# Attention on one core: the order of steps written over four rounds instead of two, with five bursts of V products

## The chip, the cores and the metric

The kernel runs on one core of a Trainium2 chip. The metric is the device time of one execution in microseconds. The median of three runs of the kernel before is 2798.07 us (2798.04 to 2798.45).

## The reference

Two attention blocks A and B with 32 heads of width 16 act on the same input x (2048 tokens, 512 features, fp32), each with its own weights, and their results are mixed by a gate of one number per token.

```python
qkv = transpose((x @ wqkv).reshape(B, S, 3, H, Dh), 2, 0, 3, 1, 4)
q, k, v = qkv[0], qkv[1], qkv[2]
p = softmax(einsum("bhqd,bhkd->bhqk", q, k) * Dh ** -0.5, axis=-1)
o = einsum("bhqk,bhkd->bhqd", p, v)
a = transpose(o, 0, 2, 1, 3).reshape(B, S, D) @ wo     # the same for b with its weights
g = sigmoid((x * gate_w).sum(-1, keepdims=True))
out = g * a + (1 - g) * b
```

## The kernel before

**Heads and rounds.** The 64 heads of A and B are worked through one after the other. A head has 16 rounds; a round is a tile of 128 keys against all 2048 queries. That makes 1024 rounds, and `r` counts them. Three kinds of work belong to them, each some rounds apart from the others:

- *Scores* (`score(r, c)`, step `e`): one matmul of 128 keys by 512 queries into a bank of `ps_st`, and one exponential on ScalarE from the bank to the tile `p` of the round. A round has four. Ahead of the exponential the maximum of each query over all keys must be known; it enters the matmul as two more rows of the operands (50 rows: 48 for the product, in which each number is split in two parts, and two for the maximum).
- *Maxima* (`max_plain`, `max_pair`, `max_rise`): another pass over the same products, 22 rounds ahead (`m = r + NT + LEAD`). A plain one (step `m`) is a matmul of 128 queries by 512 keys into a bank of `ps_m` and a reduction on VectorE into a column of `mxp`, the head's tile of partial maxima. In every second round two of the four are joined: `max_rise` (step `D`) puts the difference of two keys' products into a bank of `ps_st`, from which ScalarE makes its positive part, the tile `rise`; `max_pair` (step `A`) makes a product into `ps_m`, and VectorE adds `rise` and takes the maximum in one instruction.
- *V products* (`attend`, a digit): the exponentials times V, in quarters of a round (128 queries of each 512). Four matmuls stand side by side in the columns of the array, and the sums for a head gather in the one bank `acc`. A digit is a burst of so many quarters. When a head ends, ScalarE copies `acc` to `ev` and SyncE stores it to `od`.

**Pairs on the array.** Scores and maxima fill 48 or 50 of 128 rows, so `q_st` and `k_st` hold each head twice, at rows 0 and 64 (`HALVES`), and matmuls take the halves in turn (`rows()`, `turn`): two neighbours run at the same time. At each burst the turn is set back to the first half. `max_rise` always stands on the first half, which is where `x_st` lies.

**What sets the order.** The instructions of each engine are issued in the order of the program. The order is written out by hand as a string, `FULL`, of which each character is a step; the loop goes through it once for two rounds (`LATE` where no maxima are left). `ps_st` has four banks, `ps_m` three, `p` and `rise` have three and two buffers.

**Around the loop.** Before it stands the prologue with the projections and the first 24 rounds of maxima. In it `later` holds work with a round at which it is due: loads of V, the gate, and the output projection (`project_out`), issued ahead of the next burst. At a head's first round `load_stacks` loads the operands of the head after the next through SyncE's queue, ten DMAs. When the last maximum of a head is done, `max_split` reduces its `mxp` to `mrow` and `max_rows` transposes it and sends it through memory into the two further rows of `q_st`; two dictionaries say in which round.

Of the kernel before, what the change touches and what calls it, by code (L numbers as in the profile page):

```python
# [23 lines left out]
F32 = mybir.dt.float32  # L24
# [8 lines left out]
P = 128  # L33
# [4 lines left out]
NT = S // P  # L38
# [4 lines left out]
NH = 2 * H  # L43
ROUNDS = NH * NT
LEAD = 6
# [6 lines left out]
def gated_mha(ctx: ExitStack, tc: tile.TileContext, xT, x, wqkv_a, wo_a, wqkv_b, wo_b, gate_w, out):  # L52
    nc = tc.nc
    pe, act, dve, pool = nc.tensor, nc.scalar, nc.vector, nc.gpsimd
# [4 lines left out]
    small = ctx.enter_context(tc.tile_pool(name="small", bufs=2))  # L59
# [31 lines left out]
    def load_stacks(h, halves=HALVES):  # L91
        dma = nc.sync.dma_start
        s, hh = divmod(h, H)
        g, j = divmod(hh, HG)
        q, k = q_st[h % 3], k_st[h % 3]
        qs, ks, xs = qd[s][g], kd[s][g], xd[s][g]

        def pairs(t, step, n=S):
            v = t[0, j]
            return bass.AP(tensor=v.tensor, offset=v.offset, ap=[[n, DH], [step, 2], [1, n]])  # L100

        for b in halves:
            dma(k[b:b + 32].bitcast(F32), pairs(ks, HG * DH * S))
            dma(q[b:b + 32].bitcast(F32), pairs(qs, 0))
            dma(k[b + 32:b + 48].bitcast(F32), ks[0, j])
            dma(q[b + 32:b + 48].bitcast(F32), qs[1, j])
        if h and halves[-1] == HALVES[1]:
            x = x_st[h % 2]
            dma(x[:32].bitcast(F32), pairs(xs, HG * DH * 512, 512))
            dma(x[32:SC].bitcast(F32), xs[0, j])  # L110
# [5 lines left out]
    LOWEST = -3.4028234e38  # L116
    FIRST = NT + LEAD + 2
    mxp, rises = {}, {}
    turn = [0]

    def rows():
        turn[0] ^= 1
        return HALVES[1 - turn[0]]

    def scores_bank(m, c):
        h, t = divmod(m, NT)
        if h not in mxp:
            mxp[h] = small.tile([P, NT, 4], F32, name="mxp")
            if h:
                pool.memset(mxp[h][:, FIRST % NT if h == 1 else 0::2, 1:2], LOWEST)  # L130
        pool_ = ps_st if c == "rise" else ps_m
        ps = pool_.tile([P, 512], F32, name="ps_st" if c == "rise" else "ps_m")
        b = rows()
        q = q_st[h % 3]
        if c == "rise":
            assert b == 0
            k = x_st[h % 2][:]
        else:
            k = k_st[h % 3][b:b + SC, c * 512:(c + 1) * 512]
        pe.matmul(ps, q[b:b + SC, t * P:(t + 1) * P], k, start=True, stop=True)  # L140
        return ps, mxp[h][:, t]

    def max_plain(m, c):
        ps, o = scores_bank(m, c)
        dve.tensor_reduce(o[:, c:c + 1], ps, op=ALU.max, axis=AX.X)  # L145
# [3 lines left out]
    def max_rise(m):  # L149
        ps, _ = scores_bank(m, "rise")  # L150
        rises[m] = small.tile([P, 512], F32, name="rise")
        act.activation(rises[m], ps, AF.Relu)  # L152

    def max_pair(m):
        ps, o = scores_bank(m, 0)
        rise = rises.pop(m)
        dve.tensor_tensor_reduce(out=rise, in0=ps, in1=rise, scale=1.0, scalar=LOWEST,  # L157
                                 op0=ALU.add, op1=ALU.max, accum_out=o[:, 0:1])
# [3 lines left out]
    def max_split(h):  # L162
        parts = mxp.pop(h)
        m = small.tile([P, NT], F32, name="mrow")
        mp = small.tile([P, 2, NT], F32R, name="mparts")
        dve.tensor_reduce(m, parts, op=ALU.max, axis=AX.X)  # L166
        pool.tensor_copy(mp[:, 0], m)  # L167
        pool.tensor_tensor(mp[:, 1], m, mp[:, 0].bitcast(F32), op=ALU.subtract)
        mparts[h] = mp

    def max_rows(h):
        mt = small.tile([P, 32], F32, name="mt")
        dve.transpose(mt, mparts.pop(h).rearrange("p i t -> p (i t)").bitcast(F32))
        q = q_st[h % 3]
        r = md[h % 3]
        nc.sync.dma_start(r.rearrange("i (t a x) -> a (i t) x", a=4, x=32), mt)
        for b in HALVES:
            nc.sync.dma_start(q[b + SC:b + SC + 2].bitcast(F32), r)
# [4 lines left out]
    def score(r, c):  # L183
        h, kt = divmod(r, NT)
        if c == 0:
            pt[r] = pro.tile([P, S], F32, name="raw") if r < 2 else ppool.tile([P, S], F32, name="p")
        q, k = q_st[h % 3], k_st[h % 3]
        kk, cc = (4 * (kt % 4) + c, kt // 4) if h == NH - 1 else (kt, c)
        b = rows()
        ps = ps_st.tile([P, 512], F32, name="ps_st")  # L190
        pe.matmul(ps, k[b:b + SC + 2, kk * P:(kk + 1) * P], q[b:b + SC + 2, cc * 512:(cc + 1) * 512],  # L191
                  start=True, stop=True)
        act.activation(pt[r][:, c * 512:(c + 1) * 512], ps, AF.Exp, scale=SCALE)  # L193
# [12 lines left out]
    with tc.tile_pool(name="xs", bufs=1) as xs, tc.tile_pool(name="pro", bufs=2) as pro:  # L206
# [20 lines left out]
        def load_x(c, n):  # L227
            raw = pro.tile([P, KC, 512], F32, name="raw")
            for k in range(0, KC, n):
                nc.sync.dma_start(raw[:, k:k + n], xT[k * P:(k + n) * P, c * 512:(c + 1) * 512].rearrange(  # L230
                    "(k p) t -> p k t", p=P))
            return raw

        def split_x(c, n, raw):
            for k in range(0, KC, n):
                act.copy(xh[c][:, k:k + n], raw[:, k:k + n])  # L236
                dve.tensor_tensor(xl[c][:, k:k + n], raw[:, k:k + n], xh[c][:, k:k + n].bitcast(F32),
                                  op=ALU.subtract)
# [50 lines left out]
        def block(fn, i):  # L289
            if i < len(blocks):  # L290
                s, g, isk = blocks[i]
                fn(s, isk * DM + g * P, P)
# [5 lines left out]
        for c in range(1, NQ):  # L298
            split_x(c, 2, load_x(c, 2))
            if c < 3:  # L300
                block(load_w, c)
        ahead = [(m, c) for m in range(NT + LEAD + 2) for c in range(4)]

        def run_ahead():
# [25 lines left out]
        for t in range(NT):  # L330
# [6 lines left out]
            if t >= NT - 4:  # L337
                for c in range(2):
                    score(*divmod(2 * (t - NT + 4) + c, 4))
        turn[0] = 0  # L340
        max_rise(NT + LEAD + 2)
        assert not ahead and not pending


# [32 lines left out]
    e = core.tile([P, NT], F32, name="gate_e")  # L377
# [153 lines left out]
    later = {}  # L531
# [80 lines left out]
    def attend_next(n):  # L612
        while n:
            r, qa = divmod(done[0], 4)
            qb = min(4, qa + n)
            attend(r, qa, qb)
            done[0] += qb - qa
            n -= qb - qa

    FULL = "m3memeem3meAe2Dmeee"  # L620
    LATE = "e2ee2ee2ee2e"
    splits, rows_of = {}, {}

    load_stacks(2)
    for r in range(2, ROUNDS, 2):
        h, kt = divmod(r, NT)
        projects = []
        for rr in (r, r + 1):
            for fn, a in later.pop(rr, ()):
                if fn is project_out:  # L630
                    projects.append(a)
                else:
                    fn(*a)
        if kt == 0 and h + 2 < NH:
            load_stacks(h + 2)
        m = r + NT + LEAD
        plain = [(m, 2), (m, 3)] + [(m + 1, c) for c in range(4)]
        scored = 0
        for step in FULL if m < ROUNDS else LATE:
            if step == "e":  # L640
                score(r + scored // 4, scored % 4)
                scored += 1
            elif step == "m":
                max_plain(*plain.pop(0))
            elif step == "D":
                if m + 2 < ROUNDS:
                    max_rise(m + 2)
            elif step == "A":
                if m in rises:
                    max_pair(m)  # L650
                else:
                    max_plain(m, 0)
                    max_plain(m, 1)
            else:
                for a in projects:
                    project_out(*a)
                projects = []
                turn[0] = 0
                attend_next(int(step))
                if r in splits:  # L660
                    max_split(splits.pop(r))
                if r in rows_of:
                    max_rows(rows_of.pop(r))
        m += 1
        if m < ROUNDS and m % NT == NT - 1:
            splits[r + 2] = rows_of[r + 4] = m // NT
    attend_next(8)
    fill_only.append(True)
    for fn, *a in fill:
# [26 lines left out]
```

## Time and profile before

| | |
|---|---|
| median of three runs | 2798.07 us |
| the profiled execution | 2798.53 us, span 2796.8 us |
| TensorE busy | 2781.7 us (99%) |
| ScalarE busy | 2424.0 us (87%) |
| VectorE busy | 2363.1 us (84%) |
| GpSimd busy | 254.8 us (9%) |
| exponentials of the scores | 4088, 626 ns each by their records |
| plain maxima on VectorE | 3096, 683 ns each |
| granted TensorE clock | 0.999 |

PE is TensorE's matmuls, PEld its weight loads, ACT ScalarE, DVE VectorE, SP SyncE with its DMA queue (SPq). Records of one engine overlap where instructions follow each other closely, and ends of matmuls are modelled, so busy time alone does not say how much an engine has left; the distance between starts or ends does.

### The profile page before, as it was taken

Reading aid. Unit: us, or ns where it says so; the run is one execution under the profiler, and the core shown is the slowest. Engines: PE = TensorE matmul, PEld = TensorE weight load, DVE = VectorE, ACT = ScalarE, POOL = GpSimd, SP = SyncE. Lnnn points to the kernel's source line nnn. Section 1 sums busy time; section 2 is a strip of 40 time slices with the busy share of each in tenths; the row PEclk is TensorE's granted clock in tenths of the full one; section 3 lists DMA queues with packets and bytes.
Section 4 is the critical chain, followed back from the end, with each engine's and each line's share of the span. In section 5 each row is a group of like instructions: output and inputs, shape, how many; then the busy total and the mean of one; then the engine's idle time right before and its main releaser. Section 6 shows DMA issues by size and latency. Waiting matters only on the chain.

```text
span 2796.8 us, 65495 instructions
## 1 busy us (share of the span) xinstructions
PE 2781.7 (99%) x26176; PEld 1317.1 (47%) x26176; DVE 2363.1 (84%) x4431; ACT 2424.0 (87%) x4789; POOL 254.8 (9%) x456
## 2 busy tenths in 40 slices
PE   8999999999999999999999999999999999999999
PEld 7877544444444444444444445444444444444444
DVE  4155799999999999999999877899999999998774
ACT  3221799999999999999999977899999999998785
POOL 2010112110000000000100232000000001011201
PEclk9999999999999999999999999999999999999999
DMA  7673423333333223333432442332323333333302
GB/s 259 203 247 146 96 60 79 66 68 58 70 62 55 53 60 56 58 60 58 89 58 49 102 102 61 58 58 50 63 53 60 58 78 70 58 73 87 76 11 93
DMA packets 91126, 225.25 MB, mean 81 GB/s; under 512 B 24150, under 2 KB 34358, under 8 KB 78278
## 3 DMA queue, kind: packets, MB, share of 16 engines
q1 hardware_dynamic: 88262, 212.15, 34.0%
q0 software_dynamic: 2560, 8.91, 1.2%
q8 instruction: 206, 3.38, 0.5%
q14 instruction: 98, 0.80, 0.1%
HBM read 152.07 MB, written 68.94 MB: 79 GB/s over the span
## 4 chain that ended last, share of the span: by engine, by line
PE 98%; ACT 1%; DMA 0%; DVE 0%; SPq 0%; issue 0%
PE acc L589 38%; PE ps_m L140 26%; PE ps_st L191 13%; PE ps_st L140 8%; PE ps_st L251 6%; PE ps_st L281 3%; PE ps_m L475 3%; ACT p L193 1%; DMA raw<-in_xT 0%; PE ps_st L475 0%; PE ps_st L526 0%; PE ps_m L526 0%; DVE o_acc L527 0%; PE ps_m L513 0%; SPq L230 0%
## 5 line engine op out<-in xcount | busy, mean ns | idle before, releaser
L193 ACT ACTIVATE p<-ps_st 128x512 f32<-128x512 f32 x4088 | 2073.0, 626 | 82.7 <-PE ps_st L191 69.7
L145 DVE TENSOR_REDUCE mxp<-ps_m 128x1 f32<-128x512 f32 x3096 | 1949.8, 683 | 184.5 <-PE ps_st L191 135.2
L140 PE MATMUL ps_m<-k_st,q_st 48*128 48x512 f32 x3596 | 1353.9, 446 | 0.1
L191 PE MATMUL ps_st<-q_st,k_st 50*128 50x512 f32 x4096 | 1215.6, 426 | 0.0
L589 PE MATMUL acc<-p,vg 128*17 128x384 f32 (+1 forms) x16336 | 1182.8, 384 | 2.9 <-ACT ev L597 2.0
L140 PEld LDWEIGHTS ps_m<-k_st,q_st 48*128 48x128 f32 x3596 | 608.6, 183 | 550.0 <-DVE mxp L145 499.7
L191 PEld LDWEIGHTS ps_st<-q_st,k_st 50*128 50x128 f32 x4096 | 617.3, 184 | 200.3 <-ACT p L193 179.8
L589 PEld LDWEIGHTS acc<-p,vg 128*17 128x17 f32 x16336 | 313.9, 96 | 422.4 <-issue 399.6
L157 DVE CUSTOM_DVE_ANT_0 rise<-ps_m,rise 128x512 f32<-128x512 f32 x500 | 339.6, 679 | 0.0
L152 ACT ACTIVATE rise<-ps_st 128x512 f32<-128x512 f32 x500 | 301.8, 604 | 37.3
L140 PE MATMUL ps_st<-x_st,q_st 48*128 48x512 f32 x500 | 248.1, 496 | 0.0
L140 PEld LDWEIGHTS ps_st<-x_st,q_st 48*128 48x128 f32 x500 | 91.4, 183 | 211.6 <-ACT p L193 211.1
L167 POOL CAST mparts<-mrow 128x16 fp32r<-128x16 f32 x64 | 12.6, 197 | 1913.8 <-DVE mrow L166 1913.8
L254 ACT CAST part<-ps_st 128x512 fp32r<-128x512 f32 x64 | 37.4, 587 | 131.9 <-PE ps_st L251 117.0
L255 DVE TENSOR_TENSOR part<-ps_st,part 128x512 fp32r<-128x512 f32 x64 | 43.9, 690 | 90.3 <-ACT part L254 79.3
L475 PE MATMUL ps_m<-wo,ot 128*128 128x512 f32 (+1 forms) x354 | 91.0, 402 | 0.0
L284 ACT COPY v_st<-ps_st 128x512 f32<-128x512 f32 x32 | 18.8, 587 | 79.8 <-PE ps_st L281 70.3
L251 PE MATMUL ps_st<-xh,whi 128*128 128x512 f32 x256 | 73.0, 405 | 8.1 <-ACT xh L236 8.1
L475 PEld LDWEIGHTS ps_m<-wo,ot 128*128 128x128 f32 (+1 forms) x354 | 64.0, 188 | 20.3 <-DVE mxp L157 5.9
L251 PE MATMUL ps_st<-xh,wlo 128*128 128x512 f32 x256 | 69.9, 396 | 0.0
L251 PE MATMUL ps_st<-xl,whi 128*128 128x512 f32 x256 | 69.5, 394 | 0.0
L251 PEld LDWEIGHTS ps_st<-xh,whi 128*128 128x128 f32 x256 | 47.6, 191 | 24.7 <-ACT xh L236 10.4
(95 smaller groups left out, 814.4 us busy)
## 6 DMA issues: line engine op xcount, KB each, us to landing
k_st<-kd SPq DMA_DIRECT2D x128, 256.0 KB
q_st<-qd SPq DMA_DIRECT2D x128, 256.0 KB
qd<-part SPq DMA_DIRECT2D x32, 512.0 KB
kd<-part SPq DMA_DIRECT2D x32, 512.0 KB
k_st<-kd SPq DMA_DIRECT2D x128, 128.0 KB
q_st<-qd SPq DMA_DIRECT2D x128, 128.0 KB
od<-ev SPq DMA_DIRECT2D x63, 256.0 KB
vd<-v_st SPq DMA_DIRECT2D x32, 272.0 KB
```

What stands on the lines that cost most here:

```text
L140: pe.matmul(ps, q[b:b + SC, t * P:(t + 1) * P], k, start=True, stop=True)
L145: dve.tensor_reduce(o[:, c:c + 1], ps, op=ALU.max, axis=AX.X)
L152: act.activation(rises[m], ps, AF.Relu)
L157: dve.tensor_tensor_reduce(out=rise, in0=ps, in1=rise, scale=1.0, scalar=LOWEST, op0=ALU.add, op1=ALU.max, accum_out=o[:, 0:1])
L191: pe.matmul(ps, k[b:b + SC + 2, kk * P:(kk + 1) * P], q[b:b + SC + 2, cc * 512:(cc + 1) * 512], start=True, stop=True)
L193: act.activation(pt[r][:, c * 512:(c + 1) * 512], ps, AF.Exp, scale=SCALE)
L251: pe.matmul(ps, a[:, k], b[:, k], start=n == 0, stop=n == 3 * KC - 1)
L254: act.copy(pt[0][:, sl], ps)
L255: dve.tensor_tensor(pt[1][:, sl], ps, pt[0][:, sl].bitcast(F32), op=ALU.subtract)
L281: pe.matmul(ps, a[:, k, o:o + P], b[:, k], start=n == 0, stop=n == 3 * KC - 1)
L475: pe.matmul(ps, ot[a][:n, slot, sl], wt[b][:n, g], start=G == groups[0] and i == 0, stop=G == groups[-1] and i == 2)
L589: pe.matmul(acc[32 * c:32 * c + 17, qa * P:qb * P], v[:, 4 * a + c if final else kt, j], p[:, c * 512 + qa * P:c * 512 + qb * P], start=fi ...
```

## The change

The string `FULL` now covers four rounds with five bursts (3, 4, 3, 3, 3 quarters) in place of two rounds with three (3, 3, 2). The loop starts at round 2 as before and takes four rounds a pass, so a head is four passes and starts in the middle of one. Rises are made four and six rounds ahead of the pass's first maximum (`to_rise`), two of them with one score between, and the prologue makes two of them instead of one. What is due in the third and fourth round of a pass is issued at its ninth score (`due(r + 2)`). The stacks are loaded in the round after the first two of a head. `mxp` is made and its columns set (`new_maxima`) in the prologue for two heads and then eight rounds ahead of the head's first maximum, where it was made at its first use. `max_split` and `max_rows` go behind the first and the second burst of the pass that follows a head's last maxima.

```diff
+    def new_maxima(h):
+        mxp[h] = small.tile([P, NT, 4], F32, name="mxp")
+        if h:
+            pool.memset(mxp[h][:, FIRST % NT if h == 1 else 0::2, 1:2], LOWEST)
+
     def scores_bank(m, c):
         h, t = divmod(m, NT)
-        if h not in mxp:
-            mxp[h] = small.tile([P, NT, 4], F32, name="mxp")
-            if h:
-                pool.memset(mxp[h][:, FIRST % NT if h == 1 else 0::2, 1:2], LOWEST)
...
-        turn[0] = 0
-        max_rise(NT + LEAD + 2)
+        for i in range(2):
+            turn[0] = 0
+            max_rise(FIRST + 2 * i)
...
-    FULL = "m3memeem3meAe2Dmeee"
+    FULL = "mme3emmeem4meeemAe3emmeeem3meeemA3DeD"
...
+    load_stacks(2)
+    r = 2
+    while r < ROUNDS:
         m = r + NT + LEAD
-        plain = [(m, 2), (m, 3)] + [(m + 1, c) for c in range(4)]
+        order = FULL if m < ROUNDS else LATE
+        n = order.count("e") // 4
+        due(r)
+        if r % NT == 2 and r // NT + 2 < NH:
+            if r // NT:
+                load_stacks(r // NT + 2)
+            new_maxima(r // NT + 2)
+        plain = [(m + i, c) for i in range(4) for c in range(2 - i % 2 * 2, 4)]
+        pairs, to_rise = [m, m + 2], [m + 4, m + 6]
         scored = 0
-        for step in FULL if m < ROUNDS else LATE:
+        for step in order:
             if step == "e":
+                if scored == 8:
+                    due(r + 2)
                 score(r + scored // 4, scored % 4)
...
                 turn[0] = 0
                 attend_next(int(step))
-                if r in splits:
-                    max_split(splits.pop(r))
-                if r in rows_of:
-                    max_rows(rows_of.pop(r))
-        m += 1
-        if m < ROUNDS and m % NT == NT - 1:
-            splits[r + 2] = rows_of[r + 4] = m // NT
+                if row_ops:
+                    fn, h = row_ops.pop(0)
+                    fn(h)
+        if m < ROUNDS and (m + 4) % NT == 0:
+            row_ops += [(max_split, m // NT), (max_rows, m // NT)]
+        r += n
```

What TensorE is given in the middle of a head, before, for two rounds from `D` on (L191 are scores, L140 maxima and rises, L589 V products; the numbers name the head's stacks):

```order
L140 MATMUL ps_st<-x_st_135,q_st_2304 128x512
L140 MATMUL ps_m<-k_st_2305,q_st_2304 128x512
L191 MATMUL ps_st<-q_st_126,k_st_127 128x512 x3
L140 MATMUL ps_m<-k_st_2305,q_st_2304 128x512
L589 MATMUL acc<-p,vg 17x384 x4
L140 MATMUL ps_m<-k_st_2305,q_st_2304 128x512
L191 MATMUL ps_st<-q_st_126,k_st_127 128x512
L140 MATMUL ps_m<-k_st_2305,q_st_2304 128x512
L191 MATMUL ps_st<-q_st_126,k_st_127 128x512 x2
L140 MATMUL ps_m<-k_st_2305,q_st_2304 128x512
```

A run of six, a burst of three quarters and another run of six. Now the part of the new order that begins with the burst of four (lines are two to four higher: L192 scores, L141 maxima, L593 V products):

```order
L593 MATMUL acc<-p,vg 17x128 x4
L593 MATMUL acc<-p,vg 17x384 x4
L141 MATMUL ps_m<-k_st_2309,q_st_2308 128x512
L192 MATMUL ps_st<-q_st_126,k_st_127 128x512 x3
L141 MATMUL ps_m<-k_st_2309,q_st_2308 128x512 x2
L192 MATMUL ps_st<-q_st_126,k_st_127 128x512
L593 MATMUL acc<-p,vg 17x128 x4
L593 MATMUL acc<-p,vg 17x256 x4
L192 MATMUL ps_st<-q_st_131,k_st_132 128x512
L141 MATMUL ps_m<-k_st_2309,q_st_2308 128x512 x2
L192 MATMUL ps_st<-q_st_131,k_st_132 128x512 x3
L141 MATMUL ps_m<-k_st_2309,q_st_2308 128x512
```

The burst of four ends one round's V products and takes three quarters of the next; the two runs behind it have seven matmuls each, and in the second a new head's scores begin (its stacks are 131 and 132).

The other place is the first maximum of a new head on TensorE, with the semaphores that each instruction waits for. Before:

```order
L140 MATMUL ps_st<-x_st_130,q_st_131 128x512 [waits DMAHW2_49,DMAHW4_49,DMAHW1_49,Activation_49]
L140 MATMUL ps_m<-k_st_127,q_st_126 128x512 [waits DVE_49]
L191 MATMUL ps_st<-q_st_2304,k_st_2305 128x512 [waits Activation_49] x3
L140 MATMUL ps_m<-k_st_132,q_st_131 128x512 [waits DMAHW6_49,DMAHW5_49,DMAHW7_49,DMAHW0_49,DVE_49]
L589 MATMUL acc<-p,vg 17x384 x4
```

And now:

```order
L141 MATMUL ps_st<-x_st_130,q_st_131 128x512 [waits DMAHW3_49,DMAHW5_49,DMAHW2_49,Activation_49]
L192 MATMUL ps_st<-q_st_2308,k_st_2309 128x512 [waits Activation_49]
L141 MATMUL ps_st<-x_st_130,q_st_131 128x512 [waits Activation_49]
L141 MATMUL ps_m<-k_st_132,q_st_131 128x512 [waits DMAHW6_49,DMAHW1_49,DMAHW7_49,DMAHW0_49,DVE_49]
L141 MATMUL ps_m<-k_st_132,q_st_131 128x512 [waits DMAHW4_49,DVE_49]
L192 MATMUL ps_st<-q_st_2308,k_st_2309 128x512 [waits Activation_49]
L593 MATMUL acc<-p,vg 17x384 x4
```

The matmul that waits for the DMAs of the new head's stacks stood behind three scores and ahead of a burst; it stands now behind the second of two rises, in the middle of a run.

More of the change, by code (lines that the diff above doesn't have):

```diff
@@ L301, in gated_mha @@
                 block(load_w, c)
+        for h in range(2):
+            new_maxima(h)
         ahead = [(m, c) for m in range(NT + LEAD + 2) for c in range(4)]
@@ L618, in attend_next, with due @@
             n -= qb - qa
-    FULL = "m3memeem3meAe2Dmeee"
+    FULL = "mme3emmeem4meeemAe3emmeeem3meeemA3DeD"
     LATE = "e2ee2ee2ee2e"
[L622 to L629, printed above, removed]
+    projects, row_ops = [], []
+    def due(first):
+        for r in (first, first + 1):
+            for fn, a in later.pop(r, ()):
                 if fn is project_out:
@@ L633, in gated_mha @@
                     fn(*a)
-        if kt == 0 and h + 2 < NH:
-            load_stacks(h + 2)
+    load_stacks(2)
+    r = 2
+    while r < ROUNDS:
         m = r + NT + LEAD
-        plain = [(m, 2), (m, 3)] + [(m + 1, c) for c in range(4)]
+        order = FULL if m < ROUNDS else LATE
[7 more added lines that the diff above has]
+        pairs, to_rise = [m, m + 2], [m + 4, m + 6]
         scored = 0
-        for step in FULL if m < ROUNDS else LATE:
+        for step in order:
             if step == "e":
+                if scored == 8:
+                    due(r + 2)
                 score(r + scored // 4, scored % 4)
@@ L645, in gated_mha @@
             elif step == "D":
-                if m + 2 < ROUNDS:
-                    max_rise(m + 2)
+                k = to_rise.pop(0)
+                if k < ROUNDS:
+                    max_rise(k)
             elif step == "A":
[L649 to L653, printed above, removed]
+                max_pair(pairs.pop(0))
             else:
@@ L656, in gated_mha @@
                     project_out(*a)
-                projects = []
+                projects.clear()
                 turn[0] = 0
                 attend_next(int(step))
-                if r in splits:
-                    max_split(splits.pop(r))
-                if r in rows_of:
-                    max_rows(rows_of.pop(r))
-        m += 1
-        if m < ROUNDS and m % NT == NT - 1:
-            splits[r + 2] = rows_of[r + 4] = m // NT
+                if row_ops:
[4 more added lines that the diff above has]
+        r += n
     attend_next(8)
```

## The prediction

> **What bounds the kernel now.** I read the page first, then the stretches of the main loop, then the timeline of each engine through one pass of two rounds, and last the places where a pass takes longer.
>
> ```profile
> span 2796.8 us, 65495 instructions
> PE 98%; ACT 1%; DMA 0%; DVE 0%; SPq 0%; issue 0%
> ...
> 1000.00:1200.00 200.00, 200.00 (x2068) 85.20 (x2064) 186.43 (x356) 196.59 (x394) 5.44 (x19) 1.00 0.33 61
> 1600.00:1800.00 200.00, 200.00 (x1803) 98.69 (x1801) 156.63 (x292) 156.22 (x307) 37.31 (x49) 1.00 0.31 68
> ```
>
> The page's chain of waits is TensorE almost throughout. The lower rows are two stretches of 200 us of the main loop: busy time of PE, PEld, DVE, ACT and POOL in that order, then the granted clock, which is full. Yet ScalarE reads 98% busy in the ordinary stretch (196.59 of 200) and VectorE 93%, so all three stand close together, and how much room ScalarE has must come from its timeline. The second stretch holds output projections: there ScalarE falls to 78%. Now one pass of TensorE, two rounds long:
>
> ```profile
> 1504.34 0.84 PE L589 MATMUL acc<-p,vg 128*17 128x128 f32 x16
> 1505.12 0.50 PE L140 MATMUL ps_m<-k_st,q_st 48*128 48x512 f32 x1
> ...
> 1505.78 0.63 PE L589 MATMUL acc<-p,vg 128*17 128x256 f32 x8
> 1506.33 0.49 PE L140 MATMUL ps_st<-x_st,q_st 48*128 48x512 f32 x1
> ...
> 1506.83 0.18 PEld L191 LDWEIGHTS ps_st<-q_st,k_st 50*128 50x128 f32 x1 [0.20 <-ACT p L193]
> ...
> 1506.91 0.42 PE L140 MATMUL ps_m<-k_st,q_st 48*128 48x512 f32 x1
> 1507.26 0.84 PE L589 MATMUL acc<-p,vg 128*17 128x384 f32 x8
> 1508.03 0.49 PE L140 MATMUL ps_m<-k_st,q_st 48*128 48x512 f32 x1
> ...
> 1508.93 0.85 PE L589 MATMUL acc<-p,vg 128*17 128x128 f32 x16
> ```
>
> Start to start this gives bursts of V products of 0.78 (three quarters of a round), 0.55 (two) and 0.77 (three), and between them runs of score matmuls of 0.66 (four matmuls, two pairs), 0.93 (six, D among them) and 0.90 (six): 4.59 in all, 4.60 from one D to the next. A quarter costs 0.78 - 0.55 = 0.22, so about 0.12 of each burst is fixed; a pair costs 0.90 - 0.66 = 0.24, so 0.66 - 0.48 = 0.18 of each run is fixed. **A burst with its run thus carries about 0.30 us that has nothing to do with its work.** The rest is ScalarE:
>
> ```profile
> 1503.71 3.07 ACT L193 ACTIVATE p<-ps_st 128x512 f32<-128x512 f32 x6
> 1506.86 0.60 ACT L152 ACTIVATE rise<-ps_st 128x512 f32<-128x512 f32 x1
> 1507.36 4.02 ACT L193 ACTIVATE p<-ps_st 128x512 f32<-128x512 f32 x8
> ...
> 1508.56 2.48 DVE L145 TENSOR_REDUCE mxp<-ps_m 128x1 f32<-128x512 f32 x4 [0.30 <-PE ps_st L191]
> ```
>
> Eight exponentials take 4.02, the last 0.60 of it alone: one finishes every 3.42 / 7 = 0.49. Nine (eight and a rise) need 4.41 of 4.60, so ScalarE has 0.19 a pass; records overlap, which hides it. VectorE finishes one every (2.48 - 0.68) / 3 = 0.60, seven in 4.2, with 0.30 idle. ScalarE is not the bound, but it is close: its sixth exponential ends at 1503.71 + 3.07 = 1506.78, the weight load that waited for that PSUM bank starts 0.05 later, its matmul 0.08 after that, and the burst 0.43 after the load. That wait is the 0.03 by which this run of six is longer than the other.
>
> **The change part by part.** *Bursts.* Four rounds now hold bursts of 3, 4, 3, 3, 3 instead of two times 3, 3, 2: five for six, with the same sixteen quarters, 16 scores, 12 plain maxima, two pairs and two rises. One fixed part goes: -0.30.
>
> *Odd runs.* The runs between them are now of 6, 6, 7, 7 and 6 matmuls. Matmuls go in pairs on the two halves of the rows, so a seventh is alone. What one alone costs shows in the prologue, where three maxima stand between projections:
>
> ```profile
> 244.31 0.73 PE L140 MATMUL ps_m<-k_st,q_st 48*128 48x512 f32 x3
> 244.97 0.50 PE L281 MATMUL ps_st<-wvhi,xh 128*128 128x512 f32 x1
> ```
>
> Three take 0.66, as four do in the loop: a single one pays for the pair, 0.24. Sixteen pairs in four rounds become seventeen slots. So of the 0.30 only 0.06 is left, and over 250 passes of four rounds TensorE's own work shrinks by 15 us. The Trainium skill ("TensorE: Matmul & The Clock Gate", "Wait — 56ns, not 53.3ns?") gives 215.7 ns start to start for such a matmul; by it the extra slot would be 0.22 and TensorE's own gain 20 us. The trace has 0.24 for a pair, and decides.
>
> *ScalarE's banks.* Is the 0.06 cashed? `ps_st` has four banks, so each score waits for the exponential four places back. Follow the new order from the end of the burst of 4: it is the longest stretch without scores, and ScalarE runs dry in it. The first score behind it (e5 of sixteen) finishes its exponential 0.53 + 0.60 (the rise rows: matmul to rise, rise's length) and some 0.03 for the second of a pair later, 1.16. From there ScalarE has e5 to e15 without a gap, ten steps of 0.49 = 4.90. The next pass's e1 needs the bank of e15 (behind e15 come D, e16, D, which fill the other three): 0.05 to the load, 0.43 to the burst. Then follow a burst of three 0.77, a run of six 0.90 and the burst of four, 0.55 + 2 x 0.22 = 0.99. Sum 1.16 + 4.90 + 0.05 + 0.43 + 0.77 + 0.90 + 0.99 = **9.20 for four rounds, against 2 x 4.60 = 9.20 now.** TensorE's own work is shorter, but this loop through ScalarE is as long as what there was. It costs the 15 us again, at 0.01 either way per link; I take 0 +- 0.04 a pass, +-10 us. The rule against this change stands in the Trainium skill ("TensorEngine Tiling", "PSUM Bottleneck"): tiling speeds up TensorE, not the emptying of PSUM, which can become the limit. The rows agree that it is near: 18 x 0.49 = 8.8 of 9.2.
>
> *Where projections stand* (32 of them, in 16 of the 250 passes), ScalarE has room (156 of 200 busy) and the 0.06 is kept: -1 us. They still go ahead of a burst, one in each two rounds.
>
> *The turn of a head*, 62 times. Two passes in eight are longer now:
>
> ```profile
> 1049.57 0.49 PE L140 MATMUL ps_st<-x_st,q_st 48*128 48x512 f32 x1
> 1049.89 0.62 ACT L606 COPY ev<-acc 128x512 f32<-128x512 f32 x1
> 1054.47 0.49 PE L140 MATMUL ps_st<-x_st,q_st 48*128 48x512 f32 x1
> ...
> 1068.28 0.49 PE L140 MATMUL ps_st<-x_st,q_st 48*128 48x512 f32 x1
> 1068.98 0.46 PE L140 MATMUL ps_m<-k_st,q_st 48*128 48x512 f32 x1
> 1069.38 0.84 PE L589 MATMUL acc<-p,vg 128*17 128x384 f32 x8
> 1070.12 0.21 DVE L166 TENSOR_REDUCE mrow<-mxp 128x16 f32<-128x64 f32 x1
> ...
> 1073.05 0.50 PE L140 MATMUL ps_st<-x_st,q_st 48*128 48x512 f32 x1
> ...
> 1074.89 0.20 DVE L173 STREAM_TRANSPOSE mt<-mparts 128x32 f32<-128x32 f32 x1
> ```
>
> The first, 4.90, has the copy of `acc` on ScalarE; it is the same after (the copy stands ahead of the rises in both): 0. The second is 4.77, and all of its 0.17 lies in the run from D (1068.28) to the burst (1069.38): 1.10 for 0.93. In it stands the first maximum of the next head, which waits for four DMA semaphores besides its bank, behind a score that waits for ScalarE until the last moment. In the new order it stands behind the second D, whose bank is free before the burst ends, so TensorE's queue can get through these waits under the burst: -0.17 x 62, about -10 us; nothing, if they are not hidden. Against it, VectorE's reduction to `mrow` and its transpose (0.21 and 0.20, some 0.27 each with their gaps) now fall within one pass, at its first and second burst, where two passes shared them; their 0.5 meets 0.6 of idle time, but three `ps_m` banks let part through. I take 0.06 x 62 = +4, between 0 and +11, since the idle time is the larger of the two.
>
> *Moved loads and memset.* The ten loads of a head's stacks now follow the store of `od` and come two rounds later in the program. One set in the trace:
>
> ```profile
> 1046.01 0.56 SPq L103 DMA_DIRECT2D k_st<-kd  x1
> ...
> 1051.23 0.58 SPq L110 DMA_DIRECT2D x_st<-xd  x1
> ```
>
> Behind the copy, which ends at 1050.51, the last load would go out near 1057, and the first matmul that needs it is D at 1068.28: 11 us are left, so 0. If that cover went, SyncE's queue would hold `md` and the next head too. POOL's memset of `mxp`, 0.13 long and out of every chain, moves eight rounds earlier: 0. The rise is made four rounds ahead with two buffers; the second D needs the buffer of the pair just ahead of the last burst, 0.8 earlier: 0.
>
> **Sum.** The profiled execution took 2798.53 us, 0.46 above the median of the runs shown. Its terms are 0 - 1 - 10 + 4 = -7: 2798.5 - 7 = 2791.5, and 2791 against the median.
>
> **The rivals.**
> *A, TensorE's own work decides* (chance 0.22): ScalarE keeps up, for instance since e5 comes earlier, and the passes keep their waits of today. For it: the idle 0.19. Then 9.14 a pass, -15, and -10 at the turns: 2798 - 25 = 2773.
> *B, ScalarE's loop is longer than reckoned* (0.27): place, the scores e12, e15 and the next e1, each waiting for a bank four exponentials back. For it: its links were read to 0.01 and ten of them are the same one; it decides from 9.25 on (0.05 x 234 = 12 then outweighs the -7 by about the 5.6 named below), and 0.05 to 0.08 more a pass in 234 passes with neither gain nor loss at the turns is +12 to +19: 2810 to 2817, and 2803 to 2810 with the -7 of the turns and projections. Against it: ScalarE's pace of 0.49 is very even.
> *C, no gain at the turns* (0.13): the semaphore waits stay in the way at the new place, and all else cancels: 2798 to 2802.
> *Forecast* (0.38): 2785 to 2797.
>
> That the change does not do what it says is out: the order has five bursts.
>
> **How the numbers follow.** 0.2%, about what a measurement of this kernel can tell from no change, is 5.6 us: faster is below 2792.5. The forecast lies on both sides, 0.23 faster and 0.15 same; A is faster, 0.22; B slower, 0.27; C 0.10 same and 0.03 slower. That is 0.45, 0.25, 0.30. The range reaches from A's 2773, less 1 for its rounding, to 2810 within B; beyond it are the upper end of B and the lower half of A, 0.2 together.
>
> **What would show it.** In the new timeline: from one first D to the next 9.20 (A: 9.14; B: 9.25 and more). Runs of seven 1.14 or more. ScalarE idle once behind the burst of 4, and weight loads of `ps_st` waiting for it in the second run of seven and ahead of the first burst. The pass with the first maximum of a head no longer than its neighbours by more than 0.1. I am wrong if the runs of seven take 0.90 to 1.0 (a single matmul is then cheap, and the time nearer 2770), or if the burst of four delays scores more than 0.1 a pass.

## The result, and the profile after

The changed kernel takes 2791.84 us (2790.89 to 2793.04, 12 runs), the kernel before beside it 2798.06 us: ratio 0.9978, 95% interval 0.9971 to 0.9985. That is 6.2 us faster, 0.22%: little, but the slowest of its runs lies below the fastest of the kernel before (2797.59).

A row of the changed kernel's page, the weight loads of the scores, and a stretch of its main loop (busy time of PE, PEld, DVE, ACT, POOL):

```profile
L192 PEld LDWEIGHTS ps_st<-q_st,k_st 50*128 50x128 f32 x4096 | 621.1, 184 | 407.1 <-ACT p L194 293.9
...
1000.00:1200.00 200.00, 200.00 (x2074) 98.40 (x2070) 191.14 (x356) 196.93 (x396) 5.36 (x19) 1.00 0.30 58
```

In that stretch TensorE's and ScalarE's busy times hardly moved (VectorE's rose from 186.43 to 191.14). What did is the idle time ahead of the scores' weight loads that ends with an exponential. Before, the same group read:

```profile
L191 PEld LDWEIGHTS ps_st<-q_st,k_st 50*128 50x128 f32 x4096 | 617.3, 184 | 200.3 <-ACT p L193 179.8
```

That column must not be read as time lost. A load also counts as idle under a burst, and behind two of the five bursts now stands a score, where behind each of the three stood a maximum or a rise: the same column of the maxima's loads fell from 499.7 to 210.5. What the order costs is read from the starts. One pass of the new order on TensorE, from one first D to the next, with the starts of the two runs of seven and of the bursts behind them:

```profile
1067.03 0.49 PE L141 MATMUL ps_st<-x_st,q_st 48*128 48x512 f32 x1
...
1070.62 0.49 PE L141 MATMUL ps_m<-k_st,q_st 48*128 48x512 f32 x1
...
1071.74 0.84 PE L593 MATMUL acc<-p,vg 128*17 128x128 f32 x16
1072.51 0.49 PE L192 MATMUL ps_st<-q_st,k_st 50*128 50x512 f32 x1
...
1073.73 0.85 PE L593 MATMUL acc<-p,vg 128*17 128x256 f32 x16
1076.21 0.49 PE L141 MATMUL ps_st<-x_st,q_st 48*128 48x512 f32 x1
...
1073.30 0.18 PEld L192 LDWEIGHTS ps_st<-q_st,k_st 50*128 50x128 f32 x1 [0.26 <-ACT p L194]
```

Runs of 0.92, 0.91, 1.12, 1.22 and 0.93 with bursts of 0.77, 0.99, 0.77, 0.78 and 0.77 between them: 9.18 here. The median over the run is 9.20, against two times 4.60 before, so in the body of a head nothing was won. The first run of seven takes 1.12 (1.13 in the median), four slots' worth; the second 0.10 more, since its last score waits for its bank (the weight load at 1073.30). Over a whole head the copies of `acc` to `ev` tell more: the 17th and the 25th come 298.3 us apart before and 297.2 after, 0.13 a head less. The pass in which the next head's first maximum stands is 9.21 in the median, like its neighbours, where it was 0.17 longer; in seven heads it is 9.64 to 9.69, of which more below.

### The profile page after: what moved, and what is told of

Read it like the earlier page. It is cut to its first block, busy times and chain, and to the rows that moved or that the text cites. A ratio compares the mean times of both kernels' runs of the same rounds, so it can differ in the third digit from the quotient of the medians.

```text
span 2791.3 us, 65489 instructions
## 1 busy us (share of the span) xinstructions
PE 2774.5 (99%) x26176; PEld 1460.3 (52%) x26176; DVE 2409.5 (86%) x4431; ACT 2414.0 (86%) x4789; POOL 254.4 (9%) x456
## 4 chain that ended last, share of the span: by engine, by line
PE 98%; ACT 1%; DMA 1%; DVE 0%; issue 0%; SPq 0%
PE acc L593 37%; PE ps_st L192 22%; PE ps_m L141 20%; PE ps_st L252 6%; PE ps_st L141 5%; PE ps_st L282 3%; PE ps_m L479 3%; ACT p L194 1%; DMA raw<-in_xT 1%; PE ps_st L479 0%; PE ps_st L530 0%; PE ps_m L530 0%; DVE o_acc L531 0%; SPq L231 0%; PE ps_m L517 0%
## 5 line engine op out<-in xcount | busy, mean ns | idle before, releaser
L194 ACT ACTIVATE p<-ps_st 128x512 f32<-128x512 f32 x4088 | 2101.8, 633 | 106.9 <-PE ps_st L192 50.2
L192 PE MATMUL ps_st<-q_st,k_st 50*128 50x512 f32 x4096 | 1302.1, 438 | 0.0
L141 PE MATMUL ps_m<-k_st,q_st 48*128 48x512 f32 x3596 | 1225.4, 438 | 0.1
L593 PE MATMUL acc<-p,vg 128*17 128x256 f32 x16336 | 1134.4, 383 | 2.7 <-ACT ev L601 2.0
L192 PEld LDWEIGHTS ps_st<-q_st,k_st 50*128 50x128 f32 x4096 | 621.1, 184 | 407.1 <-ACT p L194 293.9
L141 PEld LDWEIGHTS ps_m<-k_st,q_st 48*128 48x128 f32 x3596 | 599.4, 184 | 263.5 <-DVE mxp L146 210.5
L593 PEld LDWEIGHTS acc<-p,vg 128*17 128x17 f32 x16336 | 339.7, 96 | 403.1 <-issue 331.4
L153 ACT ACTIVATE rise<-ps_st 128x512 f32<-128x512 f32 x500 | 309.8, 620 | 17.0 <-PE ps_st L192 2.6
L141 PE MATMUL ps_st<-x_st,q_st 48*128 48x512 f32 x500 | 182.1, 444 | 0.4 <-ACT p L194 0.4
L141 PEld LDWEIGHTS ps_st<-x_st,q_st 48*128 48x128 f32 x500 | 73.7, 184 | 159.2 <-ACT p L194 158.0
```

The source lines that it names most:

```text
L593: pe.matmul(acc[32 * c:32 * c + 17, qa * P:qb * P], v[:, 4 * a + c if final else kt, j], p[:, c * 512 + qa * P:c * 512 + qb * P], start=fi ...
```

## The experiments

**One score moved over a burst (even).**

```diff
-    FULL = "mme3emmeem4meeemAe3emmeeem3meeemA3DeD"
+    FULL = "mme3emmeem4meeemA3eemmeeem3meeemA3DeD"
```

> The changed order with one score moved over one burst, so that its runs are of 6, 6, 6, 8, 6 matmuls and no matmul stands alone. Theory (the loop through ScalarE's four banks sets the 9.20 us of a pass): TensorE has one slot of 0.24 less to do, but the run of eight now has five scores and stands behind a run with three; ScalarE runs dry ahead of it and TensorE waits in it for banks: about 9.5 us a pass, 2860 us or more. Rival (TensorE's own work sets the pass, the odd matmuls being what is left of the gain): 0.24 less a pass, about 8.96 us, 2735 us.

2857.56 us, 1.021 (1.0195 to 1.0226) of the kernel before; passes of 9.52. The run of eight on TensorE:

```profile
1064.91 0.50 PE L192 MATMUL ps_st<-q_st,k_st 50*128 50x512 f32 x2
...
1066.10 0.49 PE L192 MATMUL ps_st<-q_st,k_st 50*128 50x512 f32 x1 [0.21 <-ACT p L194]
...
1066.54 0.84 PE L593 MATMUL acc<-p,vg 128*17 128x256 f32 x16
```

It takes 1.63, and the row with the wait is its fifth score, which stands until the exponential four places back has ended. TensorE has a slot less to do and the kernel is 66 us slower than the changed one. So TensorE's own work does not set the pass; here the wait for one of ScalarE's four banks does. That it is the predicted loop in the changed kernel itself is read from its links, in the next section.

**ScalarE relieved, then VectorE too (after_half, before_half, after_half2, before_half2).**

```diff
-        act.activation(pt[r][:, c * 512:(c + 1) * 512], ps, AF.Exp, scale=SCALE)
+        n = 512 if r < 2 else 256
+        act.activation(pt[r][:, c * 512:c * 512 + n], ps[:, :n], AF.Exp, scale=SCALE)
...
-        dve.tensor_reduce(o[:, c:c + 1], ps, op=ALU.max, axis=AX.X)
+        dve.tensor_reduce(o[:, c:c + 1], ps[:, :256], op=ALU.max, axis=AX.X)
```

The second part is in the two kernels with a 2 only; `p` lies in three fixed tiles that are filled once. All four leave out half of the exponentials, and the two with a 2 half of the keys of a plain maximum, so none computes the reference's output.

> The changed kernel in which each exponential takes only the first 256 of its 512 columns (the other half of p holds old numbers, so the output is not the reference's). TensorE's work and order stay the same, and ScalarE has far too much room to hold anything up. Theory (TensorE's own work is 9.02 to 9.06 us a pass, and ScalarE's loop makes it 9.20): about 9.05 a pass, -0.15 x 234 = -35, and the 0.29 at the end of a head goes, -18: about 2740 us. Rival (TensorE's own work, odd matmuls included, sets the 9.20): only the end of a head gains, 2774 us. Rival (a matmul alone costs much less than a pair's 0.24 when no bank is missing): 8.8 to 8.9 a pass, 2700 us or less.

> The kernel before with the same exponentials over 256 of 512 columns. Theory (its passes of two rounds are 4.60 with 0.03 to 0.04 of waits for ScalarE): 4.56 a pass, -0.04 x 470 = -19, the end of a head -18, the turn stays: about 2761 us, so that the change without ScalarE is worth some 20 us, two slots against one burst in each four rounds (0.06 x 250 = 15), and what the turn gives. Rival (ScalarE sets the 4.60 of the order before as well): below 4.5 a pass, 2730 us or less.

With ScalarE relieved the old order takes 2756.65 us and the new one 2766.09: the expectation for the old order held (2761), that for the new one missed by 26 us (2740). Its passes are 9.17, not 9.05. A stretch of 200 us, then the last run of a pass on TensorE and VectorE there:

```profile
1000.00:1200.00 200.00, 200.00 (x2094) 96.89 (x2091) 192.80 (x360) 132.40 (x401) 5.37 (x19) 1.00 0.33 64
...
1067.29 0.50 PE L141 MATMUL ps_m<-k_st,q_st 48*128 48x512 f32 x1
...
1067.87 0.53 PE L141 MATMUL ps_m<-k_st,q_st 48*128 48x512 f32 x2
1068.33 0.84 PE L602 MATMUL acc<-p,vg 128*17 128x384 f32 x8
...
1065.96 3.15 DVE L146 TENSOR_REDUCE mxp<-ps_m 128x1 f32<-128x512 f32 x5
1069.03 0.68 DVE L158 CUSTOM_DVE_ANT_0 rise<-ps_m,rise 128x512 f32<-128x512 f32 x1
```

ScalarE is busy for 132 of 200 us and out of the way. A run of seven takes 1.13 in the median, as reckoned. But the last run, of six, takes 1.04, its pair step at the end (the second of the two at 1067.87), while VectorE (192.80 of 200) works off five reductions in a row ahead of that pair: two runs of seven with three maxima each fill the three `ps_m` banks. So I relieved VectorE as well.

> after_half (exponentials over 256 of 512 columns), and the plain maxima over 256 of 512 columns too, so that neither ScalarE nor VectorE can hold TensorE up. In after_half a pass took 9.17 instead of the 9.05 expected, and the run that ends with a pair took 1.04 for 0.90. Theory (that 0.14 is the pair's matmul waiting for one of VectorE's three banks): 9.02 to 9.05 a pass, 2728 to 2736 us. Rival (the two odd matmuls or the burst of four cost more of TensorE's own time than a slot): 9.17 a pass as in after_half, 2766 us.

> before_half with the plain maxima over 256 columns as well. Theory (TensorE's own work is 4.56 in two rounds there, and VectorE holds nothing up): 2755 us as before_half, within 4; against after_half2 that leaves TensorE's own gain by the change, 0.06 to 0.10 in four rounds, 15 to 25 us. Rival (VectorE holds up that order too): below 2748 us.

2728.12 us for the new order, as expected; 2750.43 for the old one, 5 under what was expected and 2 above the rival, so VectorE holds that order up too, by some 6 us (before_half took 2756.65). In the new one the last run is down to 0.90:

```profile
1063.87 0.50 PE L141 MATMUL ps_m<-k_st,q_st 48*128 48x512 f32 x1
...
1064.77 0.84 PE L602 MATMUL acc<-p,vg 128*17 128x384 f32 x8
```

Passes are 9.03 against 9.12. The difference of the two, 22 us, is TensorE's own gain by the change: 0.09 in each of 250 passes. In the real kernel it is hidden twice, behind ScalarE's loop (9.20) and, were that gone, behind VectorE's three banks (9.17): the two limits lie only 0.03 apart.

**The turn of a head (before_memset, before_turn, before_turn2).** All three are the old order. The first only makes `mxp` ready eight rounds ahead, and moves nothing on TensorE:

```diff
+        if kt == 2 and h + 2 < NH:
+            new_maxima(h + 2)
```

The others change the order at the turn alone, so that the first maximum of the next head stands elsewhere:

```diff
+        if m < ROUNDS and kt == 8 and m + 2 < ROUNDS:
+            order = "m3memeem3meAe2Dmmeee"    # before_turn2: "m3memeem3meAe2Dmemee"
+            plain.append((m + 2, 2))
+        elif m < ROUNDS and kt == 10:
+            order = FULL[1:]
+            plain.pop(0)
```

> The kernel before with one part of the change alone: mxp is made and set eight rounds ahead of the head's first maximum. Theory: the memset is in no chain, so 2798 us within 2, and the pass at the turn stays at 4.77. Rival (making it ready early is what shortens the turn): 4.60 and 2788 us.

> The kernel before, in which at the turn of a head alone the first maximum of the next head stands ahead of the three scores in its run instead of behind them (and so behind no score that waits for ScalarE until the last moment). Theory (the 0.17 us that this pass takes longer are semaphore waits for the new head's loads, issued behind a blocked score): the pass falls from 4.77 to about 4.62, times 62 is -9 us: 2789 us. Rival (the 0.17 us come from something else at that place: VectorE's reduction to mrow, or the memset of mxp): 2798 us, the pass stays at 4.77.

> The kernel before, with the first maximum of a head once more at another place of its run: behind D, a maximum and one score, on the second half of the rows, so that it takes all four semaphore waits for the head's loads and stands behind no score that is blocked. (In before_turn it stood on the first half and took one wait; the other four went to the last maximum of the next run, again behind a blocked score, and that run took 1.08 for 0.90.) Theory (four waits behind a blocked score cost the 0.17): the pass at the turn falls from 4.77 to about 4.60, -10 us: 2788 us. Rival (the waits cost the same wherever they stand, or the turn has another cause): 2796 to 2798 us.

before_memset takes 2798.55 us, 1.0 (0.9992 to 1.0009): that part of the change does nothing for the time. before_turn takes 2796.61, 0.9994 (0.9985 to 1.0002), where 2789 was expected. Its trace says why:

```profile
882.47 0.50 PE L140 MATMUL ps_st<-x_st,q_st 48*128 48x512 f32 x1
...
883.40 0.84 PE L589 MATMUL acc<-p,vg 128*17 128x384 f32 x8
884.17 0.50 PE L140 MATMUL ps_m<-k_st,q_st 48*128 48x512 f32 x1
...
885.25 0.84 PE L589 MATMUL acc<-p,vg 128*17 128x128 f32 x16
...
884.64 0.18 PEld L191 LDWEIGHTS ps_st<-q_st,k_st 50*128 50x128 f32 x1 [0.17 <-ACT p L193]
884.82 0.18 PEld L140 LDWEIGHTS ps_m<-k_st,q_st 48*128 48x128 f32 x1
```

The run at the turn is back at 0.93 (882.47 to 883.40), but the next one takes 1.08 (884.17 to 885.25) with a late maximum at its end: its weight load starts 0.18 after that of the score beside it. In the program the early maximum, on the first half of the rows, waits for one semaphore of the loads. The four others went to the next maximum on the second half, which in that run is the last one, behind a blocked score. The cost had moved with the waits. In the kernel before, the same two weight loads at the turn:

```profile
1068.78 0.18 PEld L191 LDWEIGHTS ps_st<-q_st,k_st 50*128 50x128 f32 x1 [0.20 <-ACT p L193]
1068.95 0.18 PEld L140 LDWEIGHTS ps_m<-k_st,q_st 48*128 48x128 f32 x1
```

The second starts 0.17 late, and in an ordinary pass the two start together (both at 1506.83). It is not the data that is late: from 1059 to 1066 the DMA engines are busy for 0.00 of the time, so the loads had landed. It is the waits themselves, and only where the matmul cannot get to them early: in before_half, with the old order and no score blocked, the pass at the turn is 4.56 like the others. In before_turn2 the early maximum stands on the second half and behind no blocked score, and takes all four. The same two runs:

```profile
880.58 0.49 PE L140 MATMUL ps_st<-x_st,q_st 48*128 48x512 f32 x1
...
881.51 0.84 PE L589 MATMUL acc<-p,vg 128*17 128x384 f32 x8
882.28 0.49 PE L140 MATMUL ps_m<-k_st,q_st 48*128 48x512 f32 x1
...
883.19 0.84 PE L589 MATMUL acc<-p,vg 128*17 128x128 f32 x16
```

0.93 and 0.91: the pass at the turn is 4.60, and the kernel takes 2789.36 us, 0.9968 (0.9955 to 0.998). This change of order at the turn alone gives the old kernel what the whole change gave (2791.84; the two intervals overlap).

**The copy of `acc` on VectorE (after_evdve, before_evdve).**

```diff
-            act.copy(ev, acc)
+            dve.tensor_copy(ev, acc)
             nc.sync.dma_start(od[G][j].rearrange("c r t -> (c r) t"), ev)
```

> The changed kernel with the copy of acc to ev on VectorE instead of ScalarE, at the end of each head. Theory (ScalarE has no room in a pass, so the 0.29 us by which the pass with the copy is longer are ScalarE's 0.49): most of the 0.29 goes, 62 times 0.2 to 0.29 is -12 to -18 us: 2774 to 2780 us. Rival (the burst behind the head's end waits for the copy as such, whichever engine makes it): the pass stays near 9.49; VectorE may have reductions queued ahead of the copy, and then it is longer: 2792 to 2810 us.

> The kernel before with the copy of acc to ev on VectorE. Theory (ScalarE has 0.19 of room in two rounds there, 0.38 in four; the 0.29 of the pass with the copy are ScalarE's): most of it goes too, -12 to -18 us: 2780 to 2786 us. Rival (the burst waits for the copy whichever engine makes it): 2798 us or slower.

Both are slower than the kernels they come from: 2800.62 and 2807.88 us, 9 and 10 more. The pass with the copy grows from 9.49 to 9.64, in the old order from 4.89 to 5.05. after_evdve at the end of a head:

```profile
1050.16 0.49 PE L141 MATMUL ps_st<-x_st,q_st 48*128 48x512 f32 x1
1050.19 0.68 DVE L158 CUSTOM_DVE_ANT_0 rise<-ps_m,rise 128x512 f32<-128x512 f32 x1
...
1050.79 0.68 DVE L610 COPY ev<-acc 128x512 f32<-128x512 f32 x1
1051.53 0.84 PE L593 MATMUL acc<-p,vg 128*17 128x384 f32 x8 [0.36 <-DVE ev L610]
```

The burst in front ends by 1050.16, but the copy starts at 1050.79, behind the pair step on VectorE, and the next burst waits for it until 1051.53. That is the rival: the one `acc` bank must be empty, whoever empties it. With the copy on ScalarE, though, that wait is the smaller part: in the changed kernel the run ahead of the burst takes 0.98 for 0.93, and the other 0.24 of the 0.29 stands in the next run (1.14 for 0.90), whose scores wait for ScalarE's banks. With ScalarE relieved (after_half) both go, and the pass with the copy is 9.17 like the rest. So the 0.29 was ScalarE's time, as expected, but moving the copy put a longer wait in its place.

**The same bursts, pairs earlier (early_pairs).**

```diff
-    FULL = "mme3emmeem4meeemAe3emmeeem3meeemA3DeD"
+    FULL = "mme3memeem4ememeAe3memeeem3emmeAe3DeD"
```

> The changed kernel with the same bursts and the same lengths of its runs, in which the pair step stands one place earlier in its run, ahead of a score, and scores and maxima take turns: the loop through ScalarE is the same, but the last run no longer ends with a pair that waits for VectorE. Theory (what is lost in the last two runs is waits for banks): 0.03 less a pass of four rounds, -8 us: 2784 us. Rival (the order within a run changes nothing): 2792 us.

2783.54 us, 0.9948 (0.9935 to 0.9962): 8.3 us under the changed kernel and faster than both. Its passes of four rounds are 9.17 in the median by the starts of D. The time was as expected, the reason was not: the last run, which was to lose its wait for VectorE, takes 0.95 as before, and the loop through ScalarE did not stay the same. The run behind the burst of four now begins with its score (e5):

```profile
1067.18 0.50 PE L192 MATMUL ps_st<-q_st,k_st 50*128 50x512 f32 x1
1067.19 0.73 PE L141 MATMUL ps_m<-k_st,q_st 48*128 48x512 f32 x2
```

In the changed kernel the maximum comes first. By the starts and ends of 197 passes without projections in each trace, the exponential of e5 ends 1.13 behind that burst where it took 1.165, and every other link of the loop is the same to 0.01 (4.90 from e5 to e15, 0.48 from there to the burst). The 0.03 that the prediction set down for "the second of a pair" is what was won. The steps were not tried one by one.

## Why the prediction was right, point by point

*The loop through ScalarE's banks, 9.20 for four rounds:* measured 9.20. Its links show in ScalarE's timeline of the changed kernel, set beside the pass on TensorE above:

```profile
1068.53 0.60 ACT L153 ACTIVATE rise<-ps_st 128x512 f32<-128x512 f32 x1
1069.01 7.67 ACT L194 ACTIVATE p<-ps_st 128x512 f32<-128x512 f32 x15
1076.74 0.60 ACT L153 ACTIVATE rise<-ps_st 128x512 f32<-128x512 f32 x1
```

Fifteen exponentials (e1 to e15) take 7.67, where 14 x 0.49 + 0.60 = 7.46 would do: 0.2 idle within them, between e4 and e5, and little else. In the median of the 197 passes e5 ends 1.165 behind the burst of four (predicted 1.16), e15 4.90 later (4.90), the next burst, behind the score that needs e15's bank, starts 0.48 after that (0.05 + 0.43), and 0.77, 0.905 and 0.99 follow (0.77, 0.90, 0.99): 9.21, the median of these passes, in which those at the ends of heads are counted too. That TensorE's own work does not decide is shown by even; that this loop does, by these links and by early_pairs, where one of them is 0.03 shorter and the pass too. Of the signs named, "runs of seven 1.14 or more" was set a little too high for the first of them (1.13).

*TensorE's own gain, 0.06 a pass or 15 us, unused:* after_half2 against before_half2 gives 0.09 and 22 us. In after_half2 a run of seven takes 1.13 and one of six 0.90: a slot costs 0.23 (predicted 0.24), so the fixed part of a burst with its run is 0.32 (0.09 + 0.23), read as 0.30 from rounded starts.

*The turn, -10:* the cause is shown by before_turn and before_turn2. In a plain head the gain is 0.15 (the pass 9.21, 4.77 + 4.59 before). In the heads with projections it is not kept: from the 31st to the 39th copy of `acc` the new kernel gains nothing on the old.

*Projections, -1:* this gain is not there. The eight passes with projections of A take 121.6 us together, 121.3 before, although the turn's gain falls into four of them; those of B 110.5 in both. Against plain heads the eight heads above lose some 1 us, and as many around the projections of B (54th to 62nd copy) 0.8; the cause is open.

*VectorE at the turn, +4:* in a plain turn it is not there; the pass is as long as its neighbours. It shows in seven turns, by work that the term did not list. The two reciprocals of eight heads' denominators (VectorE, 0.55 each, at 1216.00 and 1221.49 in one case) fell into two passes before (4.82 and 4.77, in all 0.23 above a plain turn) and fall into the pass of the turn now (9.64 to 9.69, 0.47 above a plain one). Its last run takes 1.22 for 0.95 (from 1223.04), behind five reductions in a row on VectorE. That is 0.24 lost seven times, 1.7 us. One more microsecond is lost by the end of the first head (its copy of `acc` comes 1.05 us later), which no term held. That -7 came so near to -6.2 is luck in part: the +4 was met by some 4.5 lost in other places (1.7 here, 1.8 at the projections, 1 at the start).

*Moved loads and memset, 0:* before_memset shows it for the memset. The loads were not tried apart, but in the changed kernel's trace no rise waits for a DMA (its weight loads are released by ScalarE, 158.4 us, and by nothing else above 1.1), and the set shown in the prediction, whose last load it put near 1057, has it go out at 1055.86.

*Rival A* would not have come out at 2773 even with ScalarE keeping up (after_half's 2766.09 holds some 18 us from the ends of heads, 62 x 0.29, that A did not count): its step "the passes keep their waits of today" overlooked VectorE's three banks, which hold the new order at 9.17.

## What to carry to other kernels

Cutting a fixed cost on the busiest engine pays only down to the next loop that passes through its buffers: walk that loop through the new order (issue, result, release, reuse) before counting the saving. When work runs in pairs, count slots and not instructions. Four semaphore waits cost nothing here where the matmul could get to them early and 0.17 us behind a blocked score, so look at the place of a wait in the order and not only at the number.

## What the runs showed that I had not expected

Four semaphore waits on TensorE cost 0.17 us behind a blocked score, with the data long there, and nothing in before_turn2 and before_half; and on changing the order they went to another instruction (before_turn). With ScalarE at two thirds of its load the old order is faster than the new one by 9 us (2756.65 against 2766.09), and with VectorE relieved as well slower by 22: the better order is not a property of TensorE's work alone. And emptying one PSUM bank on the less loaded engine was slower by 9 us, since that engine had a queue at that moment. Last, which of two matmuls of a pair comes first was worth 8 us (early_pairs), because one of them stood at the head of the loop.
